# Mixing the keys of two batches by 64x64 blocks in four tiles of the array

## The chip, the cores and the metric

The kernel runs on one core of one Trainium2 chip. The metric is device time in microseconds (us) of one execution; lower is better. The kernel before takes 149.82 us, the median of three runs between 149.54 and 149.90. Engines are named as in the profile: PE is TensorE (matmuls), PEld its weight loads, DVE VectorE, ACT ScalarE, POOL GpSimd, SP SyncE, which here only issues DMAs.

## What is computed

A block-mixed attention with a gated MLP behind it, for 4 batches, 8 heads, 768 tokens and 64 channels a head. `P` is an 8x8 mixing matrix for each batch and head, made by five rounds of softmax and column normalisation:

```python
k_sorted = np.einsum('bhij,bhjcd->bhicd', P, k_b)   # 8 blocks of 96 tokens, mixed
v_sorted = np.einsum('bhij,bhjcd->bhicd', P, v_b)
scores = scale * np.matmul(q_b, k_sb.transpose(0, 1, 2, 4, 3))   # block by block
attn = softmax(scores)                               # by rows, in fp32
x = np.matmul(attn, v_sb)                            # then heads side by side: [4, 768, 512]
h = np.maximum(x @ w_in, 0.0)                        # [.., 1024], halves u and v
v_n = layernorm(v)
v_s = np.einsum('ts,bsd->btd', w_spatial, v_n) + b_spatial
out = (u * v_s) @ w_out
```

Inputs and output are fp32; the matmuls work on bf16.

## The kernel before, in words

The program is a list of small units, written out by hand or by a planner in `ORDER` and run in that order: each unit emits its instructions to the engines, and every engine works through its own queue in that order, with semaphores between them. So the order of the list is the order of each queue. A unit's name is followed by its arguments: a number of a PSUM tile (0 to 3 are pairs of banks, 10 to 17 single banks), the engine that empties it (A is ACT, D is DVE, P is POOL), the batch, and then the head pair or the piece.

The units that matter here:

- `L` (line 171) loads q, k or v of a batch with a cast to bf16, issued on POOL. A partition holds 6 tokens of each head, so a piece of the load is 6 x 64 numbers.
- `PD` (290) builds, on POOL, the mixing matrix of each head as a 128x128 block matrix: each entry of `P` times a 16x16 identity. Because a partition holds 6 tokens, a block of 96 tokens is 16 partitions.
- `KT` (402, through `mixed`, 391) mixes the keys of one head pair and turns them: 12 matmuls (line 395) with 128 rows, 64 weight columns and 128 moving columns, where the two heads of the pair use the two column halves of the array. ACT or DVE then copies the result to `kT`.
- `VM` (418, matmul 422) mixes the values, and `VC` (432) moves them to blocks of 96 tokens by DMAs on SP.
- `QT` turns q on PE (first two batches). In the third and fourth, `QP` (369) packs a head pair by a copy, and `QX` (380) turns all pairs of the batch by one transposing DMA on SP.
- `SC` (446, matmul 454, exponential 459) makes the scores of four blocks of a head pair: 64 rows, so the two heads use the two row halves of the array.
- `AT` (491, matmul 500) multiplies with the mixed values; DVE divides by the sums (507, 508). `XT` or `XD` (514) turn the result into the MLP's layout.
- `VP` and `VH` (559, 578, matmul 567) make the v half of the MLP's hidden layer, in four matmuls of 512 columns or eight of 256; `ST`, `LN`, `LA` normalise it on DVE and ACT. `UP` (605, matmul 613) makes the u half.
- `SP` (620, matmul 625) mixes over tokens, with the sum `z` on DVE (631), and `GT` (637) multiplies with u. In the last batch `SH` (676, matmul 681) and `GH` (689) do this in parts, of 512 tokens (last argument 0) and 256 (last argument 1).
- `OP`, `OE`, `OS` (645 to 669) and, for the last batch, `OH`, `OI`, `OJ` (696 to 719, matmul 701) make the output, empty it and store it. `OS` and `OJ` are DMAs on SP or ACT.
- `CK` (730), `CF` (745) and `LF` (751) are a guard. The softmax leaves out its maximum; `CK` collects on DVE whether some sum went out of range, `CF` adds this up by one matmul (747) and turns it into an integer flag on DVE (748, 749), and `LF` loads the flag into a register of every engine. At `IF` in the list every engine branches on it (815): to the rest of the list (the output of the last batch), or to a safe general path that computes all anew. With these inputs it is always the former.

```python
with tc.If(st["beyond"] < 1, preferred_fallthrough_block=False, label="usual") as usual:
    run(tail)
```

Of the kernel before, what the change touches and what calls it, by code (L numbers as in the profile page):

```python
# [34 lines left out]
UP:2:A:1:0:0 ST:1:5 AT:0:2:3:0 ST:1:4 ST:1:2 UP:1:A:1:0:1 LN:1:0:6 OP:3:0:2:2 LA:1:5 LA:1:1 SC:2:2:3:1 L:v:3:0:8
SC:0:2:2:1 PD:3:4:8 LA:1:0 OP:1:0:4:2 PD:3:0:4 LA:1:3 LA:1:2 OE:A:0:2 LA:1:4 L:k:3:0:8 QP:D:3:0 VC:2:4:8:0:4 OE:A:0:4
AT:2:2:3:1 SP:0:1:3 QP:A:3:3 AT:3:2:1:0 AT:1:2:2:1 QP:A:3:1 SP:2:1:1 AT:0:2:1:1 QP:A:3:2 VM:3:A:3:1 OP:1:0:0:2
OE:D:0:0 OS:0:0:0:1:A OS:0:0:1:2:A VM:2:A:3:3 AT:3:2:0:1 SP:0:1:2 VM:1:A:3:0 GT:P:1:1 XD:2:0 VM:3:D:3:2 SP:2:1:0
VH:16:D:2:2 QX:3:0:4 KT:0:A:3:0 KT:1:D:3:2 KT:2:D:3:3 KT:3:A:3:1 XD:2:1 VH:10:D:2:0 SC:1:3:0:1 ST:2:2 SC:3:3:0:0
SC:2:3:3:1 VC:3:4:8:0:4 OS:0:4:0:1 OS:0:4:1:2 VH:11:D:2:4 VH:10:A:2:5 AT:1:3:0:1 GT:P:1:3 VH:16:D:2:3 ST:2:3 ST:2:5  # L40
GT:P:1:2 SC:2:3:1:1 SC:0:3:2:1 SC:1:3:1:0 VH:17:A:2:1 GT:D:1:0 UP:2:A:2:1:0 AT:0:3:2:1 UP:1:A:2:1:1 ST:2:1 AT:3:3:1:1
ST:2:4 AT:2:3:3:1 UP:0:A:2:0:1 ST:2:0 UP:1:A:2:0:0 VC:3:0:4:0:4 AT:3:3:0:0 LN:2:0:6 LA:2:2 OP:0:1:0:2 OE:A:1:0 LA:2:4
AT:2:3:1:0 OP:1:1:4:2 LA:2:5 SC:3:3:2:0 LA:2:0 LA:2:3 LA:2:1 SC:0:3:3:0 OP:2:1:2:2 AT:3:3:3:0 SP:0:2:1 GT:D:2:1
OE:A:1:4 XD:3:1 AT:1:3:2:0 SP:3:2:0 SP:0:2:2 CK XD:3:0 GT:P:2:0 OE:A:1:2 SP:2:2:3 VH:1:D:3:5:3 GT:D:2:3 VH:10:D:3:4
UP:3:A:3:1:1 CF:11 VH:12:A:3:2 VH:13:A:3:1 OS:1:2:0:1 OS:1:2:1:2 LF VH:16:A:3:0 GT:D:2:2 OS:1:0:0:1:A OS:1:0:1:2:A
UP:2:A:3:1:0 ST:3:1 ST:3:3 UP:0:A:3:0:0 ST:3:4 ST:3:5 OP:1:2:0:2 ST:3:2 ST:3:0 OP:3:2:4:2 LN:3:0:6 LA:3:3 OE:D:2:0
LA:3:4 OP:2:2:2:2 LA:3:0 LA:3:1 OE:A:2:2 LA:3:5 UP:0:A:3:0:1 OE:A:2:4 LA:3:2 OS:0:2:0:1 OS:0:2:1:2 SH:12:3:2:0
SH:13:3:3:0 GH:P:3:3:0 SH:16:3:0:0 GH:D:3:2:0 SH:17:3:1:0 GH:P:3:0:0 SH:16:3:1:1 SH:12:3:2:1 OS:2:4 GH:P:3:1:0
SH:13:3:3:1 OS:2:0 GH:D:3:1:1 SH:17:3:0:1 OS:1:4 GH:D:3:3:1 OS:2:2 GH:P:3:0:1 GH:P:3:2:1 IF OH:16:3:2:0:512:0:4
OI:A:3:2:0:512 OH:12:3:3:0:512:0:4 OH:13:3:0:0:512:0:4 OI:D:3:0:0:512 OI:A:3:3:0:512 OH:17:3:1:0:512:0:4  # L50
OJ:3:2:0:512:S OJ:3:3:0:512:A OI:A:3:1:0:512 OJ:3:0:0:512:S OH:16:3:4:256:512:0:4 OI:D:3:4:256:512 OH:12:3:5:0:256:0:4
OI:D:3:5:0:256 OJ:3:1:0:512:S OJ:3:4:256:512:A OH:13:3:5:256:512:0:4 OJ:3:5:0:256:S OI:D:3:5:256:512
OH:17:3:4:0:128:0:4 OH:10:3:4:128:256:0:4 OI:B:3:4:0:256 OJ:3:5:256:512:A OJ:3:4:0:256:S
# [15 lines left out]
def kernel(  # L69
# [18 lines left out]
    TB = 128 // NB  # L88
    BH = B * H
# [670 lines left out]
    def general_path():  # L760
# [88 lines left out]
```

## Time and profile before

| | |
|---|---|
| median of three runs | 149.82 us (149.54 to 149.90) |
| span of the profiled execution | 147.7 us; its own time is not listed apart from it |
| instructions | 4114 |
| granted clock of TensorE | 1.000 |
| POOL: L293 (`PD`) | 6 of 1105 ns |
| ACT: L122, keys to `kT` | 9 of 805 ns |
| DVE: L124, keys to `kT` | 7 of 947 ns |
| loads of k, 768 KB each | 14.9 us from issue to landing (median) |

The span runs from the first to the last instruction. A row of a group gives its busy time, then the mean duration of one; the chain of waits lists, in order of time, the start, the length and the work that ended last; a row of the timeline gives start, duration, engine, line, operation and names, with the idle time before it in brackets. A matmul's duration holds the way through the array, so the distances between starts, and the lengths in the chain, tell its cost in a stream. Matmuls that use different parts of the array can run side by side; "128\*64" in a row means 128 rows by 64 columns of it.

### The profile page before, as it was taken

The page shows a single profiled execution, that of the slowest core. Times are in us where ns is not written, and L with a number is a line of the kernel's source. Part 1 is how long each engine was busy: PE and PEld are TensorE (multiplying, and loading weights), DVE is VectorE, ACT ScalarE, POOL GpSimd, SP SyncE. Part 2 cuts the span into 40 slices and gives each one's busy share as a digit, 9 for nine tenths or more (in the row PEclk, how much of TensorE's full clock was granted, in tenths as well). Part 3 has the DMA queues.
Part 4 walks back from the last instruction along what each step waited for, and adds up shares of the span by engine and source line. Part 5 has one row for each costly group of instructions (what it writes and reads, how often), then busy time and mean ns, then how long its engine had stood idle before and what let it go on. Part 6 is the DMA issues. An engine that isn't in the chain of part 4 may idle for free.

```text
span 147.7 us, 4114 instructions
## 1 busy us (share of the span) xinstructions
PE 141.4 (96%) x1691; PEld 101.0 (68%) x1691; DVE 115.1 (78%) x263; ACT 85.2 (58%) x125; POOL 39.1 (26%) x44
## 2 busy tenths in 40 slices
PE   6997999999999999999999999999999999999991
PEld 2466777857776667776877678768866876854760
DVE  3878899979987978867869879899558989846741
ACT  5357998988789447658793328756640046160040
POOL 6701994410000006991002640000002100004630
PEclk9999999999999999999999999999999999999999
DMA  2999999999999999899999999503602507007856
GB/s 60 278 204 205 204 207 201 208 225 243 227 233 231 204 200 269 131 177 211 206 202 175 213 239 278 132 0 83 28 0 60 190 2 284 0 2 266 307 210 228
DMA packets 37013, 25.93 MB, mean 176 GB/s; under 512 B 16704, under 2 KB 34112, under 8 KB 36992
## 3 DMA queue, kind: packets, MB, share of 16 engines
q0 software_dynamic: 14432, 12.19, 51.9%
q1 hardware_dynamic: 21552, 11.88, 33.8%
q10 hardware_dynamic: 1008, 1.57, 2.8%
q8 instruction: 14, 0.23, 0.6%
q14 instruction: 7, 0.06, 0.1%
HBM read 24.78 MB, written 6.29 MB: 210 GB/s over the span
## 4 chain that ended last, share of the span: by engine, by line
PE 82%; DMA 8%; DVE 5%; POOL 2%; issue 1%; ACT 1%; POOLq 0%; DVEq 0%
PE ps L625 16%; PE ps L567 15%; PE ps L613 14%; PE ps L651 11%; DMA k_in<-in_k_dram 8%; PE ps L681 5%; PE ps L500 4%; PE ps L395 4%; PE ps L701 4%; PE ps L454 4%; PE ps L422 3%; DVE x_sb L508 2%; PE ps L326 1%; PE ps L536 1%; PE ps L530 1%; DVE vb L124 1%
## 5 line engine op out<-in xcount | busy, mean ns | idle before, releaser
L642 POOL TENSOR_TENSOR gt<-z,u_sb 128x768 bf16<-128x768 f32 x7 | 11.4, 1642 | 68.0 <-DVE z L631 54.7
L459 ACT ACTIVATE ex_all<-ps 96x768 bf16<-96x768 f32 x32 | 23.7, 805 | 5.0 <-PE ps L454 4.1
L625 PE MATMUL ps<-wspT,v_sb 128*128 128x384 bf16 x144 | 25.0, 326 | 0.0
L567 PE MATMUL ps<-w_in_sb,xT 128*128 128x256 bf16 (+1 forms) x176 | 23.8, 283 | 0.0
L613 PE MATMUL ps<-xT,w_in_sb 128*128 128x384 bf16 x128 | 23.0, 326 | 0.0
L128 ACT ACTIVATE u_sb<-ps 128x768 bf16<-128x768 f32 x16 | 13.0, 811 | 17.3 <-PE ps L613 17.2
L508 DVE TENSOR_TENSOR x_sb<-ps,rec_all 96x512 bf16<-96x512 f32 x32 | 22.0, 687 | 1.1
L625 PEld LDWEIGHTS <-v_sb 128*128 128x128 bf16 x144 | 13.5, 98 | 8.4
L567 PEld LDWEIGHTS <-xT 128*128 128x128 bf16 x176 | 16.2, 98 | 4.0
L651 PE MATMUL ps<-w_out_sb,gt 128*128 128x256 bf16 x144 | 16.9, 273 | 0.0
L613 PEld LDWEIGHTS <-w_in_sb 128*128 128x128 bf16 x128 | 12.0, 98 | 7.0
L587 DVE BATCH_NORM_STATS2 stats<-v_sb 128x6 f32<-128x512 bf16 x24 | 16.2, 675 | 0.6 <-ACT v_sb L128 0.5
L122 ACT COPY o_sb<-ps 128x1024 f32<-128x1024 f32 (+2 forms) x11 | 8.9, 830 | 12.6 <-PE ps L701 9.3
L631 DVE TENSOR_TENSOR z<-ps,b_bc 128x768 f32<-128x768 f32 x12 | 11.5, 954 | 5.9 <-PE ps L625 5.1
L651 PEld LDWEIGHTS <-gt 128*128 128x128 bf16 x144 | 13.8, 98 | 2.0
L500 PEld LDWEIGHTS <-ex_all 96*128 96x128 bf16 x256 | 11.1, 97 | 2.6
L500 PE MATMUL ps<-vb,ex_all 96*128 96x65 bf16 x256 | 12.4, 193 | 0.1
L122 ACT CAST vm<-ps 128x768 bf16<-128x768 f32 x9 | 6.8, 807 | 9.7 <-PE ps L422 6.6
L694 POOL TENSOR_TENSOR gt<-z,u_sb 128x512 bf16<-128x512 f32 (+1 forms) x5 | 5.2, 1046 | 21.5 <-DVE z L687 21.5
L507 DVE RECIPROCAL rec_all<-ps 96x8 f32<-96x8 f32 x32 | 6.3, 196 | 5.5 <-PE ps L500 5.3
L130 DVE TENSOR_SCALAR v_sb<-ps 128x512 bf16<-128x512 f32 (+1 forms) x12 | 8.7, 727 | 1.7 <-PE ps L567 1.5
L236 PE MATMUL ps<-warm 128*128 128x512 bf16 (+3 forms) x38 | 8.5, 386 | 1.3 <-DVE warm L210 1.3
(100 smaller groups left out, 199.9 us busy)
## 6 DMA issues: line engine op xcount, KB each, us to landing
v_in<-in_v_dram POOLq DMA_DIRECT2D x4, 768.0 KB, 16.0
k_in<-in_k_dram POOLq DMA_DIRECT2D x4, 768.0 KB, 14.9
vb<-vm SPq DMA_DIRECT2D x24, 99.0 KB, 4.8
q_in<-in_q_dram POOLq DMA_DIRECT2D x3, 768.0 KB, 11.6
out_dram<-o_sb SPq DMA_DIRECT2D x9, 256.0 KB, 2.3
out_dram<-o_sb SPq DMA_DIRECT2D x4, 512.0 KB, 5.9
out_dram<-o_sb ACTq DMA_DIRECT2D x5, 256.0 KB, 2.3
ws_in<-in_moe_w_spatial_dram POOLq DMA_DIRECT2D x2, 576.0 KB, 18.9
```

What stands on the lines that cost most here:

```text
L122: nc.scalar.copy(out=out, in_=in_)
L128: nc.scalar.activation(out=out, in_=in_, func=AF.Relu)
L459: nc.scalar.activation(out=e_tile(b, hp, ih).rearrange("p h (x g) -> p h x g", g=G), in_=t[0:BLK, :, 0:HW].rearrange("p h (g x) -> p h x g ...
L500: nc.tensor.matmul(t[:, hh, ii * VW:ii * VW + D + 1], lhsT=e[:, c:c + 128], rhs=vb[b % 2][:, ih * NI + ii, 2 * hp + hh, 0:D + 1], start=Tr ...
L508: nc.vector.tensor_mul(out=x_sb[:, hp].rearrange("p i (h d) -> p h i d", h=2), in0=tv[:, :, :, 0:D], in1=_raw_ap(rec, 0, [rec.ap[0], [NI, ...
L567: nc.tensor.matmul(t[:, x, c:c + DH // parts], lhsT=st["xT", b][:, n // 3, kc, (n % 3) * 128:(n % 3 + 1) * 128], rhs=w_in_sb[:, kc, DH + c ...
L587: nc.vector.bn_stats(out=stats, in_=st["v_sb", b, n])
L613: nc.tensor.matmul(t[:, x, 0:HW], lhsT=w_in_sb[:, kc, mc * 128:(mc + 1) * 128], rhs=st["xT", b][:, ih, kc, :], start=(kc == 0), stop=(kc = ...
L625: nc.tensor.matmul(t[:, x, 0:HW], lhsT=st["v_sb", b, n][:, mc * 128:(mc + 1) * 128], rhs=wspT[:, 3 * x:3 * x + 3, n, :], start=(n == 0), s ...
L631: nc.vector.tensor_add(out=z.rearrange("p (x c) -> p x c", x=2), in0=t[:, :, 0:HW], in1=b_bc.rearrange("p (x c) -> p x c", x=2),)
L642: eng.tensor_mul(out=gt, in0=st["z", b, mc], in1=u)
L651: nc.tensor.matmul(t[:, x, c:c + w], lhsT=st["gt", b, mc][:, (n0 + x) * 128:(n0 + x + 1) * 128], rhs=w_out_sb[:, mc, c:c + w], start=(mc = ...
```

## The change

For the third and fourth batches k is loaded in another layout: a partition holds 12 tokens of one head, the first 64 partitions one head of a pair and the last 64 the other, so a piece is 12 x 64 numbers. A block is then 8 partitions, and the mixing matrix of a head is 64x64 (`PN` on POOL, from `prep8`, which `PS` and `PY` make on PE and DVE out of the same `P`; `M8` prepares two small constants on POOL). `KP` replaces two `KT`: 48 matmuls of 64 rows, 64 weight columns and 64 moving columns, for two head pairs, four at a time in the four 64x64 tiles of the array, each of the four into another bank. `PD` stays for the values. In the odd head pairs of these batches the two heads change places (`half`), so that all four tiles are used; q has to follow, and `QP` copies such a pair in two halves.

The order is new behind the first batch's attention; up to there `M8` is the only unit put in. The number of units of each kind stays, but for eight `KT` that become four `KP`, the new `M8`, `PS`, `PY` and two `PN`, and six `VH` that become `VP`. Many units go to another engine or place. `CF`, which stood in the fourth batch's `VH`, now stands behind the last `SH`, and `LF` behind that. `SH` gets an argument to split its matmuls, which isn't used, and the general path gets the new units.

```diff
...
-UP:3:A:3:1:1 CF:11 VH:12:A:3:2 VH:13:A:3:1 OS:1:2:0:1 OS:1:2:1:2 LF VH:16:A:3:0 GT:D:2:2 OS:1:0:0:1:A OS:1:0:1:2:A
...
-SH:13:3:3:0 GH:P:3:3:0 SH:16:3:0:0 GH:D:3:2:0 SH:17:3:1:0 GH:P:3:0:0 SH:16:3:1:1 SH:12:3:2:1 OS:2:4 GH:P:3:1:0
-SH:13:3:3:1 OS:2:0 GH:D:3:1:1 SH:17:3:0:1 OS:1:4 GH:D:3:3:1 OS:2:2 GH:P:3:0:1 GH:P:3:2:1 IF OH:16:3:2:0:512:0:4
...
+SC:0:0:0:0 L:v:1:0:8 PD:1:0:4 VB:15:D:0:3 SC:3:0:1:0 AT:1:0:2:0 SC:0:0:2:1 AT:2:0:3:0 SC:3:0:0:1 PD:1:4:8 M8
...
+ST:0:4 VP:12:A:0:1 ST:0:3 VH:10:A:0:5 L:wsb VP:13:A:0:0 PD:3:4:8 ST:0:5 WT:12:A:1 VH:16:A:0:2 ST:0:1 ST:0:0 WT:13:A:0
+PS:12 SC:0:1:3:0 PY:D VC:1:0:4 SC:2:1:0:0 WT:17:D:2 ST:0:2 LN:0:0:6 UP:1:A:0:0:0 BI AT:3:1:1:0 AT:0:1:0:0 UP:2:A:0:1:1
...
+AT:1:1:3:0 SP:0:0:1 AT:1:1:1:1 QP:A:2:3 VM:2:A:2:2 L:k:2:0:4 QP:A:2:0 SP:3:0:3 VM:0:D:2:3 QP:A:2:2 PN:2:0:4 QP:A:2:1
+PN:3:0:4 XD:1:0 VM:1:D:2:0 XD:1:1 GT:P:0:2 SP:2:0:0 KP:3:0:AA:2:1 UP:1:A:1:1:0 QX:2:0:4 VH:17:D:1:2 KP:2:0:AA:2:0
...
+LA:3:1 OE:A:2:2 LA:3:0 LA:3:3 LA:3:2 LA:3:5 OE:A:2:0 SH:11:3:1:0 SH:17:3:2:0 SH:12:3:0:0 GH:P:3:2:0 SH:14:3:0:1
+GH:D:3:0:0 OS:2:4 OS:0:2:1:2 GH:P:3:0:1 SH:16:3:3:0 GH:D:3:1:0 SH:10:3:2:1 GH:D:3:3:0 SH:12:3:1:1 OS:2:2 GH:P:3:2:1
+SH:17:3:3:1 CF:15 GH:D:3:1:1 GH:D:3:3:1 LF OS:1:0:1:2:A OS:2:0 OS:0:4:0:1 IF OH:16:3:2:0:512:0:4 OI:A:3:2:0:512
...
+        if what == "k" and int(a[0]) >= KB:
...
+            nc.gpsimd.dma_start(
+                out=st["k", b][:, lo:hi],
+                in_=_raw_ap(k, (b * H + 2 * lo) * S * D, [[GR * D, 128], [2 * S * D, hi - lo], [1, GR * D]]),
+            )
...
+    def u_PS(ps):
...
+        for i in range(NI):
+            for hh in range(2):
+                nc.tensor.matmul(
+                    parts[hh * 64:hh * 64 + 64, i], lhsT=spread8[:, i * NB:(i + 1) * NB].rearrange("p j t -> p (j t)"),
+                    rhs=turned_p[:, hh, :, KB * HP:], start=True, stop=True,
+                )
...
+    def u_PN(b, lo, hi):
+        b, lo, hi = int(b), int(lo), int(hi)
+        n = hi - lo
+        nc.gpsimd.tensor_mul(
+            out=pn(b)[:, lo:hi].rearrange("p h (i t) -> p h i t", t=TR),
...
+    def half(b, hp, hh):
+        lo = 64 * (hh ^ (hp & 1) if b >= KB else hh)
+        return slice(lo, lo + 64)
...
+    def u_KP(ps0, ps1, eng, b, m):
+        b, m = int(b), int(m)
+        ts = [ps_tile(ps0), ps_tile(ps1)]
+        for n in range(GR):
+            for row in range(2):
+                g = (n + G * row) % GR
+                for o in range(2):
+                    rows = slice(64 * row, 64 * row + 64)
+                    nc.tensor.matmul(
+                        ts[o][half(b, o, row), g // G, (g % G) * 64:(g % G) * 64 + 64],
+                        lhsT=st["k", b][rows, 2 * m + o, g * D:(g + 1) * D], rhs=pn(b)[rows, 2 * m + o, :],
+                        start=True, stop=True,
+                    )
+        for o in range(2):
+            to = turned("kT", b, 2 * m + o)[:, 0:S].rearrange("p (x b g) -> p b x g", b=2, g=G)
+            copy(eng[o], to, ts[o][:, :, 0:HW].rearrange("p b (g x) -> p b x g", g=G))
```

More of the change, by code (lines that the diff above doesn't have):

```diff
@@ L374, in u_QP @@
                 "p (k g h d) -> p k g h d", k=HP, g=G, h=2)
-        copy(
-            eng, st["qp", b][:, hp].rearrange("p g h d -> p h g d"),
-            st["q", b][:, 2 * hp:2 * hp + 2].rearrange("p h (g d) -> p h g d", g=G),
-        )
+        to, of = st["qp", b][:, hp], st["q", b][:, 2 * hp:2 * hp + 2].rearrange("p h (g d) -> p h g d", g=G)
+        if half(b, hp, 0).start == 0:
+            copy(eng, to.rearrange("p g h d -> p h g d"), of)
+        else:
+            for hh in range(2):
+                copy(eng, to[:, :, 1 - hh], of[:, hh])
     def u_QX(b, lo, hi):
@@ L452, in u_SC @@
             for hh in range(2):
-                rows = slice(hh * 64, hh * 64 + 64)
+                rows = half(b, hp, hh)
                 nc.tensor.matmul(
@@ L471, in u_SM @@
             for hh in range(2):
-                rows = slice(hh * 64, hh * 64 + 64)
+                rows = half(b, hp, hh)
                 nc.tensor.matmul(
```

119 lines of the change are left out of this document (74 added, 45 removed).

## The prediction

> **What bounds the kernel now.** I read the page first, then the busy time by stretches, then the chain of waits in order of time.
>
> ```profile
> span 147.7 us, 4114 instructions
> PE 141.4 (96%) x1691; PEld 101.0 (68%) x1691; DVE 115.1 (78%) x263; ACT 85.2 (58%) x125; POOL 39.1 (26%) x44
> PE 82%; DMA 8%; DVE 5%; POOL 2%; issue 1%; ACT 1%; POOLq 0%; DVEq 0%
> ```
>
> The chain that ended last is TensorE for 82% of the span. The three timed runs have a median of 149.82 us; the profiled execution is listed with its span alone, so about 2.1 us lie around the span, and I leave them as they are. The second view gives, for each stretch, its length and then the busy time of PE, PEld, DVE, ACT and POOL.
>
> ```profile
> 24.80:56.00 31.20, 31.15 (x405) 21.73 (x405) 26.81 (x57) 23.35 (x35) 2.27 (x3) 1.00 1.25 222
> 56.00:87.00 31.00, 31.00 (x368) 22.96 (x367) 24.05 (x48) 19.73 (x28) 15.35 (x12) 1.00 1.18 204
> 87.00:115.00 28.00, 28.00 (x346) 20.82 (x344) 23.19 (x49) 15.06 (x21) 1.64 (x1) 1.00 0.48 89
> 115.00:131.40 16.40, 16.40 (x134) 12.81 (x132) 13.76 (x35) 5.74 (x9) 0.01 (x1) 1.00 0.27 99
> 131.40:139.20 7.80, 7.80 (x50) 4.69 (x48) 4.47 (x9) 1.71 (x2) 3.75 (x3) 1.00 0.69 262
> 139.20:147.70 8.50, 5.22 (x37) 3.08 (x34) 3.38 (x9) 2.02 (x4) 1.41 (x2) 1.00 0.54 199
> ```
>
> From 24.8 us until the last matmul PE has work at every moment (31.15 of 31.20, then all of it), at a granted clock of 1.00, and every other engine has room: DVE, the fullest, is busy 26.81 of the first 31.20 us. So a microsecond of matmul taken out there is a microsecond of time, unless something makes PE wait; and any wait of PE is paid in full. The part up to 24.8 us (softmax rounds, first loads) keeps its order of units in the change, so I count nothing there. The chain in order of time then prices each kind of matmul:
>
> ```profile
> 27.68 0.79 PE ps L395 x24
> 31.05 1.83 PE ps L567 x8
> 46.27 1.95 PE ps L625 x12
> 52.85 0.65 PE ps L422 x4
> 56.98 1.46 PE ps L395 x48
> 58.44 1.41 PE ps L613 x8
> 60.72 0.62 PE ps L454 x24
> 62.31 1.30 PE ps L613 x8
> 72.03 0.45 PE ps L454 x16
> 87.33 1.46 PE ps L395 x48
> 100.95 0.24 PE ps L500 x8
> 119.44 0.10 PE ps L747
> 119.54 2.73 PE ps L567 x24
> 131.41 7.80 PE ps L681 x48
> 139.21 5.22 PE ps L701 x36
> ```
>
> **Matmuls removed.** The k mixing (L395) of the third and fourth batches goes, 48 matmuls each. Between the rows of 24 and 48, 24 more take 1.46 - 0.79 = 0.67 us: 27.9 ns each, 55.8 ns for two, which lie in two column halves of the array and run together. 96 x 27.9 = 2.68 us off the path. The rest of those rows, 0.12 us, is the price of going into another tiling; the eight L613 matmuls behind it take 1.41 instead of 1.30, so going out costs 0.11. For the scores (L454, two row halves) 8 more take 0.62 - 0.45 = 0.17 us, 21.2 ns each, and 0.11 us is left over again. I take 0.105 us for a crossing.
>
> **Matmuls added.** Each KP issues 48 matmuls of 64 rows by 64 columns with 64 moving columns, in groups of four that use four different tiles and four different banks. The nearest row for such a width is L500: 65 moving columns, one at a time, 0.24/8 = 30 ns. If four tiles run together a group costs 30 ns, twelve groups 0.36 us, four KP 1.44 us. Both weights and data must keep that pace. This row (shortest, median, longest) tells of the weights:
>
> ```profile
> L395 PE MATMUL ps<-pd,k_in x192: 219/219/243, 15.4 to 88.6; 128*64 128x128 bf16 x192
> ```
>
> The first matmul of a unit takes 243 - 219 = 24 ns more, as it waits for its own 64 weight columns; all later loads are hidden. 24 ns fits under 30 ns if the tiles load side by side, with little room. The lower end is 30 ns; the upper ends are two tiles at a time (60 ns a group, 2.88 us) and one at a time (120 ns, 5.76 us). I take 30 ns, since both pairs that the trace shows (two columns, two rows) overlap fully.
>
> [...]
>
> PS adds eight matmuls of 32 rows and 16 moving columns. Four of 32 rows and 64 columns took
>
> ```profile
> L267 PE MATMUL ps<-p_t,spread 32*128 32x64 bf16 x4 | 0.3, 190 | 0.5 <-DVE mask L224 0.5
> ```
>
> with their run-out; four pairs at 30 ns are 0.12 us (0.24 if one at a time). Crossings between tilings, counted in the two orders from the first VM of the second batch: 28 before; after, 33, since the four KP and PS stand apart from each other. 5 x 0.105 = 0.53 us. All other unit kinds keep their number; VP in place of VH is the same 2048 columns in fewer instructions. So PE's own work changes by -2.68 + 1.44 + 0.12 + 0.53 = **-0.59 us**.
>
> **The flag at the end.** The new order moves CF. CF is one matmul (L747), a reduction and a cast on DVE (L748, L749); LF then has every engine load the flag, and IF branches on it. Before, CF stands at 119.44 and PE has 24 more matmuls (to 122.27) to cover the flag:
>
> ```profile
> 119.92 0.14 DVE L748 TENSOR_REDUCE ends<-ps 1x1 f32<-1x5 f32 x1
> 120.09 0.14 DVE L749 CAST flag<-ends 1x1 int32<-1x1 f32 x1
> ```
> ```profile
> L752 PEldq TENSOR_LOAD <-flag x1: 493/493/493, 120.3 to 120.3; - x1
> ```
> ```profile
> L815 PEldq COMPARE_BRANCH  x1: 481/481/481, 137.4 to 137.4; - x1
> L815 DVEq COMPARE_BRANCH  x1: 84/84/84, 139.8 to 139.8; - x1
> ```
>
> After, CF comes behind the very last SH, and then PE's queue holds LF, the branch and the output matmuls (L701): nothing to run while it waits. Behind LF wait also DVE's copies of the output, SP's last two OS and all OJ, and one OS of ACT. CF's two DVE steps stand behind all that DVE has to do for the SH units; the steps from one DVE start to the next are in
>
> ```profile
> 135.40 0.69 DVE L687 TENSOR_TENSOR z<-ps,b_bc 128x512 f32<-128x512 f32 x1 [0.67 <-PE ps L681]
> 136.01 0.68 DVE L694 TENSOR_TENSOR gt<-z,u_sb 128x512 bf16<-128x512 f32 x1
> 136.69 0.69 DVE L687 TENSOR_TENSOR z<-ps,b_bc 128x512 f32<-128x512 f32 x1
> 138.86 0.42 DVE L687 TENSOR_TENSOR z<-ps,b_bc 128x256 f32<-128x256 f32 x1 [0.36 <-POOL gt L694]
> 139.20 0.41 DVE L694 TENSOR_TENSOR gt<-z,u_sb 128x256 bf16<-128x256 f32 x1
> ```
>
> a wide z 0.61, a wide gt 0.68, a narrow z 0.34. The 48 SH matmuls take 7.80 us in all, wide units 1.30, narrow 0.65. In the new order the wide ones are first, second, third and fifth, so the last wide one ends 5.85 us after SH begins, and its z starts 0.10 later, as 135.40 does behind 131.41 + 3.90 = 135.31. On DVE: z at 5.95, gt 6.56, narrow z 7.24, wide gt 7.58, narrow z 8.26 and 8.60, CF's reduction at 8.94. From the reduction to PE's load 120.3 - 119.92 = 0.38, the load 0.49, the branch 0.48: the first output matmul at 10.29 in place of 7.80. PE stands for **2.5 us**. Lower end: DVE has no backlog but the last z (7.90, so the reduction at 8.24) and the branch costs nothing as its target is at hand (0.08 on DVE): 8.24 + 0.38 + 0.49 = 9.11, 1.3 us. Upper end 3.2 us: two waits of a z for POOL, 0.36 us each, as the row of 138.86 has one. I take the middle, as each of its steps has its row.
>
> **Other waits.** The transposed q of the third batch (QX) is now asked for later. Before, its copies and its way were
>
> ```profile
> L122 ACT COPY qp<-q_in x7: 823/833/850, 46.8 to 77.0; 128x768 bf16<-128x768 bf16 x7
> ```
> ```profile
> qT<-qp SPq DMA_TRANSPOSE x1, 6.4
> ```
> ```profile
> L382 SPq DMA_TRANSPOSE qT<-qp x2: 3856/4064/4273, 51.8 to 80.2; - x2
> ```
>
> from 51.8 with 6.4 us to landing, and the first scores at 60.72 had 2.5 us in hand. After, three of its four copies stand on ACT behind the VM copy of a unit that PE begins at about 51.7, and PE wants the result at about 61.8 (the units of the new order added up from 31.1, where the two orders part, each at its row of the chain: L567 0.87 us, L613 1.30, L625 1.95, L422 0.33, L500 0.24, L454 0.17, L395 0.34 and the transposes at its pace, KP 0.36, and the crossings). Two of the four copies are cut in halves; an instruction more costs between 0 and 0.4 us, and I take 0.2. 52.1 + 0.83 (VM's copy, of the same size) + 0.83 + 0.83 + 1.03 puts QX at 55.6 and its landing at 62.0. I add 0.1 us, with 0 to 1.0 as ends. The new loads of k are half as many pieces of twice the length; they are needed no earlier than before, so I count nothing for them. Uncovered they would cost at most the M8, PN and PD steps put ahead of loads on POOL,
>
> ```profile
> L293 POOL TENSOR_TENSOR pd<-mask,prep_sb 128x512 bf16<-128x512 bf16 x6 | 6.5, 1105 | 7.6 <-ACT prep_sb L122 7.6
> ```
>
> 1.1 us for a PD and, by its size, about half for a PN or for M8; POOL is 26% busy, which hides them. SP's two OS behind LF send 0.75 MB more into the last stretch, which moved 199 GB/s at a DMA share of 0.54: 0 to 0.7 us, and I take 0, as the last OJ is issued over 5 us later.
>
> Sum: -0.59 + 2.5 + 0.1 = +2.0, so **151.8 us**. A measurement of this kernel can tell about 0.3%, 0.45 us, from no change.
>
> **Rivals.** *The flag does not hold PE.* If LF and the branch were passed before the flag's chain matters, only PE's own work would count: 149.82 - 0.59 = 149.2, faster. For it speaks that no wait on the flag shows on PE's path before; against it, that PE's load came 0.2 us after the cast began, as soon as there was a flag to read, and no matmul is left to cover it. The point that decides is PE's idle time between L747 and L701: under 0.15 us it is faster. Chance 0.09.
> *A short flag.* DVE arrives without backlog and the branch is free (1.3 us), the rest as bounded low, or PE loses fewer crossings: 149.82 - 0.59 + 1.0 to 1.3 = 150.2 to 150.5; around this lies no change. Chance 0.10.
> *Four tiles don't run together.* Two at a time add 2.88 - 1.44 = 1.4 us, 153.2; one at a time 4.3, 156.1. For it: no four-tile row in the trace, and 24 ns of weights against 30 ns. Against: the full overlap of both kinds of pairs. [...] Chance 0.05 for two at a time and 0.02 for anything slower, as the score pairs already run closer together than that.
>
> The forecast keeps 0.74, with its own range 150.5 to 153.0. The range of 149.9 to 153.0 takes in the short flag as well. Faster 0.09, within 0.3% 0.10, slower 0.81.
>
> **What would show it.** Right: no L395 in the last two batches, KP groups of 48 at about 0.36 us plus a crossing, PE work down by about 0.6 us, and between L747 and the first L701 a hole of some 2.5 us that ends with PE's flag load, with L748 late behind z and gt of DVE. Wrong: the L701 matmuls right behind L681 (then faster), KP at 0.7 us or more (then later still), or new PE idle time around 62 us or 80 us from q, v or vb that lands late.

## The result and the profile after

The changed kernel takes 159.97 us (median of four runs, 159.27 to 160.71) against 149.77 us: a ratio of 1.067, 95% interval 1.059 to 1.074. The forecast of 151.8 us had the sign and two of the mechanisms; 8 us of the time were not in it. A median here is over all runs of a kernel; a ratio leaves out, on both sides, the executions over 1.5% longer than the fastest of the same kernel, and the kernel before has such executions too, most of them at 153 to 155 us.

From here on the lines are those of the new file: AT is L570 (it was L500), VC L505, QX L435, the mixing KP L466, SH L753, CF L819 to L821, the flag's load L824, the branch L894, the output matmuls L773. The profiled execution took 159.27 us. Four lines of its page:

```profile
span 157.5 us, 4269 instructions
PE 145.3 (92%) x1767; PEld 99.1 (63%) x1767; DVE 114.8 (73%) x265; ACT 83.8 (53%) x126; POOL 45.5 (29%) x50
PEclk9999999999999999968999999999999999999699
PE 81%; DVE 7%; DMA 4%; POOL 2%; issue 2%; ACT 1%; DVEq 0%; POOLq 0%
```

PE was 96% busy and is 92%; the granted clock, full in every slice before, drops in two places, slices 18 and 38 of 40 (from about 67 and 146 us); and the 4% of DMA in the chain are the values `vb<-vm`, which had no share in it before (the 8% there were a load of k). The stretches (length, then busy time of PE, PEld, DVE, ACT, POOL, then the granted clock, DMA share and GB/s) say where:

```profile
24.80:56.00 31.20, 31.06 (x418) 21.86 (x415) 25.89 (x56) 24.97 (x39) 6.32 (x7) 1.00 1.22 220
56.00:87.00 31.00, 28.32 (x388) 20.77 (x387) 21.59 (x45) 16.94 (x25) 10.85 (x9) 0.94 0.95 164
87.00:115.00 28.00, 28.00 (x387) 20.21 (x386) 22.66 (x45) 15.37 (x22) 3.83 (x2) 1.00 0.46 92
115.00:135.30 20.30, 20.30 (x141) 13.04 (x140) 16.27 (x41) 6.17 (x9) 6.44 (x4) 1.00 0.49 142
135.30:143.30 8.00, 8.00 (x52) 4.70 (x49) 4.61 (x9) 1.01 (x1) 2.20 (x2) 1.00 0.36 134
143.30:157.50 14.20, 7.15 (x38) 3.49 (x37) 4.60 (x13) 2.02 (x4) 1.05 (x1) 0.87 0.54 190
```

Two stretches lost, the others are as full as before. I also added up, from the starts of all matmuls from 25 us on, the distance from each to the next beyond what a stream needs at full clock: 0.8 us before, 11.1 us after. The last matmul starts 9.5 us later (153.7 against 144.2), so PE's own work became 0.8 us less; the time went into two holes.

**The first hole, 66 to 72 us.** PE's timeline in the third batch, with what it waited for in brackets:

```profile
65.78 0.20 PE L570 MATMUL ps<-vb,ex_all 96*128 96x65 bf16 x1
66.41 0.19 PE L570 MATMUL ps<-vb,ex_all 96*128 96x65 bf16 x1 [0.44 <-DMA vb<-vm]
68.09 0.19 PE L570 MATMUL ps<-vb,ex_all 96*128 96x65 bf16 x1 [1.48 <-DMA vb<-vm]
69.03 0.44 PE L570 MATMUL ps<-vb,ex_all 96*128 96x65 bf16 x5 [0.75 <-DMA vb<-vm]
69.28 1.90 PE L637 MATMUL ps<-w_in_sb,xT 128*128 128x256 bf16 x8
```

The first AT of the third batch has its scores, but the mixed values come block by block from VC's DMAs. The starts lie 3.2 us further apart than the stream needs. In the kernel before the same eight matmuls ran without a wait:

```profile
63.45 0.41 PE L500 MATMUL ps<-vb,ex_all 96*128 96x65 bf16 x8
```

After the hole the eight matmuls of L637 take 1.90 us where eight of the kind took 1.04: until about 71.7 us they start 213 ns apart instead of 109, at half clock (granted clock 0.50 from 68.5 to 71.8 us), another 1.1 us.

**The second hole, 143 to 150 us.** PE and then DVE around the flag; the flag's load and the branch on PE:

```profile
143.27 0.17 PE L819 MATMUL ps<-bad,ones 128*1 128x5 bf16 x1
146.45 3.57 PE L773 MATMUL ps<-w_out_sb,gt 128*128 128x512 bf16 x9 [3.01 <-DVE gt L766]
150.50 3.44 PE L773 MATMUL ps<-w_out_sb,gt 128*128 128x512 bf16 x27 [0.48 <-issue]
```
```profile
141.84 0.69 DVE L759 TENSOR_TENSOR z<-ps,b_bc 128x512 f32<-128x512 f32 x1 [0.56 <-POOL gt L766]
144.63 0.43 DVE L759 TENSOR_TENSOR z<-ps,b_bc 128x256 f32<-128x256 f32 x1 [0.23 <-POOL gt L766]
144.97 0.14 DVE L820 TENSOR_REDUCE ends<-ps 1x1 f32<-1x5 f32 x1
145.14 0.14 DVE L821 CAST flag<-ends 1x1 int32<-1x1 f32 x1
```
```profile
L824 PEldq TENSOR_LOAD <-flag x1: 487/487/487, 145.3 to 145.3; - x1
```
```profile
L894 PEldq COMPARE_BRANCH  x1: 395/395/395, 145.9 to 145.9; - x1
```

The bracket names DVE's gt as the releaser, but PE sat on its own flag load until 145.8 and its branch until 146.3: this is the flag's chain, 3.2 us from start to start. Behind it the first nine output matmuls take 3.57 us, six of them at half clock, 427 ns instead of 216 between starts (granted clock 0.50 from 147.0 to 150.3 us), and then there is a stop that the profile puts down to "issue", 0.7 us by the starts. A fetch of 16 KB of code ran just before it, from 147.8 to 149.1 us, but no run shows that the stop was for code. Together 5.2 us.

### The profile page after: what moved, and what is told of

Its sections match the earlier page's. It is cut to its first block, busy times and chain, and to the rows that moved or that the text cites. A ratio compares the mean times of both kernels' runs of the same rounds, so it can differ in the third digit from the quotient of the medians.

```text
span 157.5 us, 4269 instructions
## 1 busy us (share of the span) xinstructions
PE 145.3 (92%) x1767; PEld 99.1 (63%) x1767; DVE 114.8 (73%) x265; ACT 83.8 (53%) x126; POOL 45.5 (29%) x50
## 4 chain that ended last, share of the span: by engine, by line
PE 81%; DVE 7%; DMA 4%; POOL 2%; issue 2%; ACT 1%; DVEq 0%; POOLq 0%
PE ps L695 15%; PE ps L683 13%; PE ps L637 13%; PE ps L721 10%; PE ps L250 6%; PE ps L773 4%; DMA vb<-vm 4%; PE ps L570 4%; PE ps L524 3%; PE ps L492 3%; PE ps L448 2%; POOL gt L766 2%; DVE x_sb L578 2%; PE ps L377 2%; PE ps L753 2%
## 5 line engine op out<-in xcount | busy, mean ns | idle before, releaser
L712 POOL TENSOR_TENSOR gt<-z,u_sb 128x768 bf16<-128x768 f32 x11 | 18.5, 1698 | 63.3 <-DVE z L701 57.7
L637 PE MATMUL ps<-w_in_sb,xT 128*128 128x256 bf16 (+1 forms) x148 | 23.9, 312 | 0.0
L683 PE MATMUL ps<-xT,w_in_sb 128*128 128x384 bf16 x128 | 23.7, 328 | 0.0
L125 ACT COPY o_sb<-ps 128x1024 f32<-128x1024 f32 (+2 forms) x10 | 8.1, 807 | 23.1 <-PE ps L773 13.4
L131 ACT ACTIVATE v_sb<-ps 128x512 bf16<-128x512 f32 (+1 forms) x13 | 8.2, 630 | 18.9 <-PE ps L637 18.9
L637 PEld LDWEIGHTS <-xT 128*128 128x128 bf16 x148 | 14.3, 100 | 6.2
L570 PE MATMUL ps<-vb,ex_all 96*128 96x65 bf16 x256 | 13.0, 195 | 2.8 <-DMA vb<-vm 2.7
L131 ACT ACTIVATE u_sb<-ps 128x768 bf16<-128x768 f32 x15 | 12.2, 812 | 5.8 <-PE ps L683 5.4
L570 PEld LDWEIGHTS <-ex_all 96*128 96x128 bf16 x256 | 11.5, 99 | 5.7 <-issue 3.0
L133 DVE TENSOR_SCALAR v_sb<-ps 128x512 bf16<-128x512 f32 x10 | 6.9, 691 | 7.7 <-PE ps L637 6.8
L127 DVE COPY o_sb<-ps 128x1024 f32<-128x1024 f32 (+3 forms) x8 | 5.9, 740 | 6.7 <-PE ps L773 6.1
L250 PE MATMUL ps<-warm 128*128 128x512 bf16 (+3 forms) x38 | 9.6, 419 | 1.3 <-DVE warm L224 1.3
```

The lines of the kernel that those rows point to most:

```text
L131: nc.scalar.activation(out=out, in_=in_, func=AF.Relu)
L250: nc.tensor.matmul(t[:, 0, 0:int(w)], lhsT=warm[:, 0:128], rhs=warm[:, 0:int(w)], start=True, stop=True)
L570: nc.tensor.matmul(t[:, hh, ii * VW:ii * VW + D + 1], lhsT=e[:, c:c + 128], rhs=vb[b % 2][:, ih * NI + ii, 2 * hp + hh, 0:D + 1], start=Tr ...
L637: nc.tensor.matmul(t[:, x, c:c + DH // parts], lhsT=st["xT", b][:, n // 3, kc, (n % 3) * 128:(n % 3 + 1) * 128], rhs=w_in_sb[:, kc, DH + c ...
L683: nc.tensor.matmul(t[:, x, 0:HW], lhsT=w_in_sb[:, kc, mc * 128:(mc + 1) * 128], rhs=st["xT", b][:, ih, kc, :], start=(kc == 0), stop=(kc = ...
L712: eng.tensor_mul(out=gt, in0=st["z", b, mc], in1=u)
```

## The experiments

They are told as e1 to e18, in the order in which the question moved. Lost time at a place is always the sum of distances between starts, as above. Of the order list the edits show only the units that change, with some of their neighbours; the rest of each line is left out.

### The flag, and the parts by themselves: e1 to e4

e1 puts only the test back to an early place in the changed kernel:

```diff
-VP:14:A:3:1 GT:P:2:3
+VP:14:A:3:1 CF:15 GT:P:2:3
-VP:16:A:3:4 OS:1:2:0:1
+VP:16:A:3:4 LF OS:1:2:0:1
-SH:17:3:3:1 CF:15 GH:D:3:1:1 GH:D:3:3:1 LF
+SH:17:3:3:1 GH:D:3:1:1 GH:D:3:3:1
```

> The changed kernel with two units moved: CF to behind the fourth batch's VP of tile 1, LF to behind its VP of tile 4, so that matmuls cover the flag. My theory: the hole of 3.1 us between CF's matmul and the first output matmul, and the half-clock matmuls and the second stop behind it (another 2.2 us), come from the flag alone: about 154.7 us in place of 160.0, with the L773 matmuls behind L753 within 0.9 us (the last wide gt of DVE ends 0.8 us after the last L753 began to drain). Rival: it is DVE and POOL, which finish z and gt too late in the last batch, so that PE stands there anyway: at most 1 us is gained, 159 us or more.

154.76 us, ratio 1.029 (1.022 to 1.036): 5.2 us won, and the output matmuls follow SH with two stops of 0.3 and 0.1 us. The theory held: the late test is the cause of the second hole and of what follows it. The first hole stayed.

e2 leaves the order of before and changes the mixing alone (KT to KP with M8, PS, PY, PN and the new loads):

```diff
-KT:1:A:2:0 KT:2:D:2:1 KT:3:A:2:3 KT:0:D:2:2
+KP:1:2:AD:2:0 KP:0:3:DA:2:1
-KT:0:A:3:0 KT:1:D:3:2 KT:2:D:3:3 KT:3:A:3:1
+KP:0:3:AA:3:0 KP:1:2:DD:3:1
```

> The order of the kernel before, with only the blocks changed: two adjacent KP in the place of the four KT of the third and of the fourth batch, the new loads of k, M8, PS, PY and PN put where they fit, all else in its old place. My theory: the blocks themselves are a small gain and the new order is the loss. PE work: two times 1.46 us of L395 go, two times (2 x 0.40 + 0.11) come, and PS with its crossings costs 0.33: -0.8 us, so 149.0 us. Rival: the halved copies of q, the extra POOL steps or the new loads make PE wait for q, k or vb as in the changed kernel: 151 us or more.

164.76 us, ratio 1.095 (1.089 to 1.102). The theory fell, by almost 16 us. The hole at vb is larger than in the whole change (3.3 and 1.8 us, and half clock to 75 us), and PE's branch takes 5.2 us, though the flag was loaded 17 us before it.

e3 is the other half, the new order with the old KT:

```diff
-KP:3:0:AA:2:1
+KT:3:A:2:2 KT:0:A:2:3
-KP:2:0:AA:2:0
+KT:2:A:2:0 KT:0:A:2:1
-KP:1:3:DD:3:1
+KT:1:D:3:2 KT:3:D:3:3
-KP:3:0:DA:3:0
+KT:3:D:3:0 KT:0:A:3:1
```

> The new order with the old mixing: each KP is two KT again, k is loaded whole in the old layout, and M8, PS, PY and PN are gone. My theory: the late values (PE waiting for vb at the third batch's first AT) and the late flag belong to the order: both holes stay, 160 to 161 us. Rival: the blocks bring the first hole, since two of four q copies are halved and QX comes later: without them the hole of 3 us at the third batch's first AT is under 1 us, and the time 157 us or less.

156.67 us, ratio 1.048 (1.040 to 1.055). The rival's numbers came out: 0.6 us lost at vb, no half clock there; the second hole is whole, 3.2 us. It looked as if the new code, not the order alone, made vb's delay what it is; e16 below takes that back in part, as the order with KT loses 2.4 us there too.

e4 is e1 with two loads later:

```diff
-L:wo VH:16:A:1:5 L:q:3:0:8
+L:wo VH:16:A:1:5
-L:k:3:0:4 VH:13:A:1:3
+VH:13:A:1:3
-GT:P:0:1 SC:0:2:3:1
+GT:P:0:1 L:q:3:0:8 L:k:3:0:4 SC:0:2:3:1
```

> As the kernel with the early flag, and the loads of q and k of the fourth batch are issued about 4 us later, behind the last GT of the first batch, so that the values of the third batch (VC) share the DMA engines with the load of w_out alone. My theory: these loads delay VC; the hole at the third batch's first AT shrinks from 3.2 us to 1 us or less and its half-clock stretch (1.1 us) goes: about 151.5 us. Rival: VC is late because it is queued behind the transposed q (QX): the hole stays at 2.5 us or more, and the time is that of the early flag alone, about 154.7 us.

152.57 us, ratio 1.018 (1.010 to 1.025), 0.7 us lost at vb. It looked as if the theory of the loads held; e13 below takes that back.

### Addresses: e5 to e12

What do all kernels with the new code have in common that e3 lacks? Their transposing DMAs (XD, QX), which stand ahead of VC in SP's queue, are slower. Counted from the packet records: in the kernel before and in e3 the packets of 256 bytes run at up to about 1110 in a microsecond, in the others at about 830, with 13 to 17% of the packets over 22 ns instead of 1%. The new constants (`prep8`, `spread8`, `mask8`: 128, 512 and 32 bytes a partition) stand ahead of `vm`, the load tiles, `qT`, `x_sb` and `xT`, and shift them all. Before, these start at a multiple of 256 bytes; after, at 160 modulo 256 (`vb`, at 192 modulo 256 before, is shifted too).

e5 and e7, e8 first tried a grid of 64 bytes: mask8 takes 64 bytes instead of 32, in the changed kernel, in e1 and in e2. e6 goes the other way: one unused tile of 32 bytes in the kernel before.

```diff
-    mask8 = const.tile([128, TR], BF16, name="mask8")
+    mask8 = const.tile([128, 32], BF16, name="mask8")[:, 0:TR]
```
```diff
+    pad32 = const.tile([128, 16], BF16, name="pad32")
     vm = const.tile([128, G, H, VW], BF16, name="vm")
```

> The changed kernel with one number changed: the tile mask8 is declared 32 elements wide instead of 8 (the rest unused), so that it takes 64 bytes of each partition instead of 32. In the changed kernel every tile allocated behind mask8 (vm, vb, the load tiles, qp, qT) starts at an address of 32 modulo 64; in the kernel before all of them start at a multiple of 64, and here they do again. Theory (addresses off the 64-byte grid slow the transfers into those tiles, QX's transposing ones from about 1110 to about 830 packets of 256 bytes in a microsecond, so VC behind them is late): the transposing transfers run at about 1100 packets in a microsecond again, the PE time lost before the third batch's mixing falls from 3.2 us to under 1 us, without half clock behind it: 155 to 156.5 us. Rival (the new layout of k, the halved copies or the earlier q load delay VC): transfers stay at about 830, 159 to 161 us.

> The kernel before with an unused tile of 32 bytes a partition allocated ahead of vm, and nothing else: all tiles behind it start at 32 modulo 64. Theory (addresses): transposing transfers fall to about 830 packets in a microsecond, VC and vb of the third batch land 1.5 us or more later than before, and PE loses 1 to 5 us ahead of the third batch's mixing: 151 to 156 us. Rival (addresses don't matter): 149.8 us, transfers at about 1110.

> The changed kernel with the wide mask8 and with the general-path test early (CF:15 behind VP:14:A:3:1, LF behind VP:16:A:3:4, as in the run with the early test alone, 154.8 us). Theory (addresses delay VC, the late test the rest): both holes are gone, 150.0 to 151.0 us. Rival (addresses don't matter): 154 to 155.5 us.

> The order of the kernel before with the four-tile mixing of k (the run with the blocks alone, 164.8 us) and the wide mask8. Theory (addresses): the 5 us lost before the third batch's mixing and the half clock behind them go, some 8 to 11 us; what is left is the branch of 5.2 us ahead of the output matmuls if it stays: 153 to 156 us with that branch, 148.7 to 150.0 us without it. Rival (the four-tile mixing itself or k's layout delays VC): 163 to 166 us.

e5 159.52 us (ratio 1.066), e7 155.55 (1.040, interval 1.035 to 1.045), e8 164.14 (1.095): nothing won, the grid of 64 bytes fell. But e6, the kernel before with 32 unused bytes, takes 156.76 us, ratio 1.048 (1.041 to 1.055), and stops at the very place. From the list of its waits (total, times, longest):

```profile
PE ps L501 <- DMA vb<-vm: 4.0, 3, 2.5
```

So addresses do cost 7 us here, in a program that is otherwise the same; a multiple of 64 (192 modulo 256 in e5, e7 and e8) is not enough. In e6 not all of the transposing DMAs ahead of VC are slow, but the last of them alone (25% of its 1536 packets over 22 ns): VC's first packet moves from 59.15 to 60.05 us. e9, e10 and e12 give mask8 128 bytes, so that those tiles start at a multiple of 256 again ("on the grid" from here on), in the changed kernel, in e1 and in e2; e11 puts 256 unused bytes into the kernel before.

```diff
-    mask8 = const.tile([128, TR], BF16, name="mask8")
+    mask8 = const.tile([128, 64], BF16, name="mask8")[:, 0:TR]
```
```diff
+    pad256 = const.tile([128, 128], BF16, name="pad256")
     vm = const.tile([128, G, H, VW], BF16, name="vm")
```

> The changed kernel with mask8 declared 64 elements wide (128 bytes), so that the new tiles take 768 bytes and every tile behind them starts at a multiple of 256 bytes again, as in the kernel before (there 256 modulo 512, here 0). Theory (a transposing transfer is slowed when its pieces of 256 bytes lie off the 256-byte grid: in the kernel before and in the run with the order alone none of these packets takes over 22 ns, in the shifted kernels about a fifth do, 33 to 58 ns): transposing packets at about 1100 in a microsecond again, PE time lost before the third batch's mixing under 1 us: 155 to 157 us. Rival (something else of the four-tile mixing holds them up, or any shift does): about 830 packets, 159 to 161 us.

> The same with the general-path test early, as in the run with the early test alone (154.8 us). Theory (256-byte grid): both holes gone, 150.0 to 151.5 us. Rival (not the grid): 154 to 156 us.

> The kernel before with an unused tile of 256 bytes instead of 32 (which cost 7 us): the tiles behind it move and stay on the 256-byte grid. Theory (grid): 149.5 to 150.2 us, no slow transposing packets. Rival (any shift of the addresses, or a grid of 512 bytes): 153 to 157 us.

> The order of the kernel before with the four-tile mixing of k (164.8 us with the tiles off the grid), tiles on the 256-byte grid. Theory (grid): no stop of over 1 us before the third batch's mixing; 153 to 156 us if the branch ahead of the output matmuls still takes over 5 us, 148.7 to 150 us if it doesn't. Rival (the four-tile mixing or k's layout itself): 162 to 166 us.

| tiles start at, modulo 256 | kernels | packets over 22 ns, 110 to 140 us |
|---|---|---|
| 0 | before, e3, e9 to e18 | 0 to 2.4% |
| 32 | e6 | 25% |
| 160 | after, e1, e2, e4 | 26 to 29% |
| 192 | e5, e7, e8 | 26 to 28% |

e11 takes 150.15 us, ratio 1.001 (0.996 to 1.005): a shift by 256 bytes costs nothing, one by 32 bytes 7 us. No run has a start at 128 modulo 256, so a grid of 256 bytes and one of 128 are not told apart. e12 takes 155.97 us against 164.76 without the grid, e10 152.87 (ratio 1.019, 1.014 to 1.024) against 154.76, e9 159.18 (1.055, 1.048 to 1.062) against 159.97 (1.067, 1.059 to 1.074). The packets are as the theory has them in every kernel. The times of e9 and e10 are not: they were to lose under 1 us at vb and lost 2.1 and 2.6 us. In e10:

```profile
66.62 0.19 PE L570 MATMUL ps<-vb,ex_all 96*128 96x65 bf16 x1 [0.87 <-DMA vb<-vm]
68.22 0.31 PE L570 MATMUL ps<-vb,ex_all 96*128 96x65 bf16 x5 [1.40 <-DMA vb<-vm]
```

VC starts about a microsecond sooner on the grid (first packet 59.6 us against 60.7 in the changed kernel) and is late all the same. There was a second cause.

### What VC meets: e13, e16, e17, e18

e13 is e4 on the grid (its edit and that of e9 together), e16 the same with KT for KP: e3 with CF, LF and the two loads at the places of e4.

```diff
-L:wo VH:16:A:1:5 L:q:3:0:8
+L:wo VH:16:A:1:5
-L:k:3:0:8 VH:13:A:1:3
+VH:13:A:1:3
-GT:P:0:1 SC:0:2:3:1
+GT:P:0:1 L:q:3:0:8 L:k:3:0:8 SC:0:2:3:1
```

> The changed kernel with its tiles on the 256-byte grid, the general-path test early, and the loads of q and k for the fourth batch moved behind GT:P:0:1. Theory (with the grid and the test mended, what is left before the third batch's mixing is VC sharing the DMA engines with those loads): the 2.6 us lost there at 152.9 us shrink to under 1 us: 149.3 to 150.8 us. Rival (the loads don't matter, VC is late of itself): 152 to 153.5 us.

> The new order with the old mixing of k (KT), tiles where the kernel before has them, the general-path test early and the loads of q and k for the fourth batch behind GT:P:0:1: the same as e13 without the blocks. Theory (the blocks save 0.5 to 1 us of PE work when nothing covers it): 150.0 to 151.5 us, 0.5 to 1 us above e13. Rival (the blocks save nothing, or cost): the same as e13 or below.

e13 took 154.76 us (1.030, 1.023 to 1.037), e16 153.59 (1.024, 1.021 to 1.028), with 2.7 and 2.4 us lost at vb. The theory of both fell (149.3 to 150.8 and 150.0 to 151.5 us), and e13's time lies above its rival's too (152 to 153.5). The loads of q and k are not what makes VC late, and e4's gain has no explanation of mine. e16 has no blocks, no new tiles and no slow packets and still loses 2.4 us, so the new code is not needed for the hole. What the four tiles are worth, e16 could not settle: with equal losses (4.5 us each) the last matmul starts 1.3 us sooner with them (147.0 against 148.3), but the medians say the opposite.

That leaves the third load, w_out. In the kernel before, VC's first DMA is issued at 57.59 us and w_out's load at 59.79, 2.2 us behind (first row from SP's timeline, second from POOL's); after, both at the same moment:

```profile
57.59 5.70 SPq L435 DMA_DIRECT2D vb<-vm  x8
```
```profile
59.79 0.82 POOL L194 DMA_DIRECT2D w_out_sb<-in_moe_w_out_dram  x1
```
```profile
55.20 4.09 SPq L435 DMA_TRANSPOSE qT<-qp  x1
59.38 6.23 SPq L505 DMA_DIRECT2D vb<-vm  x8
```
```profile
59.36 0.81 POOL L208 DMA_DIRECT2D w_out_sb<-in_moe_w_out_dram  x1
```

In the packet records of the changed kernel VC moves 64 packets in the microsecond from 61, then 5 and 0, while w_out moves 25, 158 and 188; in the kernel before VC has moved 367 by 62 us and w_out 11. e17 moves the load back (in e10, behind POOL's `PD`, and the two others behind GT:P:0:1); e18 moves it forward in the kernel before, by one POOL operation:

```diff
-GT:P:0:0 L:wo VH:16:A:1:5 L:q:3:0:8
+GT:P:0:0 VH:16:A:1:5
-GT:P:0:3 PD:3:0:4 ST:1:5
+GT:P:0:3 PD:3:0:4 L:wo ST:1:5
```
```diff
-GT:P:0:2 SC:1:2:3:0 VH:17:D:1:3 L:wo
+L:wo GT:P:0:2 SC:1:2:3:0 VH:17:D:1:3
```

> The changed kernel on the 256-byte grid with the early test (152.9 us) and w_out's load moved behind PD:3:0:4 of POOL (about 62.6 instead of 59.1 us), q's and k's for the fourth batch behind GT:P:0:1. Theory (VC's packets share the DMA engines with w_out's, which start as VC does): vb of the third batch lands in time, PE loses under 1 us there instead of 2.6: 149.5 to 151.0 us, unless w_out then comes late for the first output matmuls at about 70 us, which would cost up to 1 us more. Rival (VC is late whatever is loaded beside it): 152.3 to 154.8 us, 2 us or more lost at the same place.

> The kernel before with w_out's load moved one POOL operation forward (ahead of GT:P:0:2: issued at about 58.2 instead of 59.8 us, 0.6 us behind VC's issue instead of 2.2), nothing else. Theory (w_out's load beside VC): PE loses 1 to 3 us ahead of the third batch's mixing, waiting for vb: 151.5 to 154 us. Rival: 149.8 us.

Against e13, e17 moves w_out's load and nothing else. e17: 151.29 us, ratio 1.011 (1.007 to 1.016), a little over the 149.5 to 151.0 expected. With the load at 61.76 the third batch's AT run without a wait:

```profile
61.76 0.81 POOL L208 DMA_DIRECT2D w_out_sb<-in_moe_w_out_dram  x1
```
```profile
65.53 0.41 PE L570 MATMUL ps<-vb,ex_all 96*128 96x65 bf16 x8
65.77 1.04 PE L637 MATMUL ps<-w_in_sb,xT 128*128 128x256 bf16 x8
66.64 0.40 PE L570 MATMUL ps<-vb,ex_all 96*128 96x65 bf16 x8
```

e18: 155.70 us, ratio 1.033 (1.027 to 1.040), more than the 151.5 to 154 expected, for one load 1.6 us sooner:

```profile
58.21 0.82 POOL L194 DMA_DIRECT2D w_out_sb<-in_moe_w_out_dram  x1
```
```profile
64.29 0.19 PE L500 MATMUL ps<-vb,ex_all 96*128 96x65 bf16 x1 [0.62 <-DMA vb<-vm]
66.46 0.22 PE L500 MATMUL ps<-vb,ex_all 96*128 96x65 bf16 x1 [1.98 <-DMA vb<-vm]
67.65 0.44 PE L500 MATMUL ps<-vb,ex_all 96*128 96x65 bf16 x5 [0.97 <-DMA vb<-vm]
```

Taken away in the one kernel and made in the other, the hole goes and comes with w_out's load. That w_out's load can make the hole, and that moving it can take it away, is shown. That it alone decides is not. In e3 the load is issued 0.9 us behind VC and in e4 beside it, and they lost only 0.6 and 0.7 us. And the execution of e11 that was profiled took 153.49 us, though the program is the kernel before with a harmless shift, has no slow transposing packets, and issues the load 1.9 us behind VC:

```profile
57.73 6.32 SPq L436 DMA_DIRECT2D vb<-vm  x8
```
```profile
59.64 0.81 POOL L195 DMA_DIRECT2D w_out_sb<-in_moe_w_out_dram  x1
```
```profile
65.85 0.31 PE L501 MATMUL ps<-vb,ex_all 96*128 96x65 bf16 x5 [2.28 <-DMA vb<-vm]
```

PE stops for vb at the same place, and half clock follows. So the order of before stands close to this edge itself, and neither the grid nor the place of the load settles a single execution.

### Clock and code: e15, e14

e15 is e9 with 12 useless matmuls for PE to run while it waits for the flag:

```diff
-SH:17:3:3:1 CF:15 GH:D:3:1:1
+SH:17:3:3:1 CF:15 DM:13:12:512 GH:D:3:1:1
```

> The changed kernel on the grid with the late test (159.2 us) and 12 useless matmuls of 512 columns behind CF's, which PE runs while it would wait for the test. Theory (PE's clock is halved behind a hole of about 3 us because PE was idle): the output matmuls behind the branch take 216 ns from the first on, 1.5 to 2.7 us are won: 156.5 to 157.8 us, and any stop for code in the middle stays. Rival (the half clock comes of something else, such as the branch): 158.7 to 160 us.

156.89 us, ratio 1.040 (1.035 to 1.044), 2.3 us under e9. PE's timeline from CF on:

```profile
142.94 2.76 PE L250 MATMUL ps<-warm 128*128 128x512 bf16 x12
146.03 5.37 PE L773 MATMUL ps<-w_out_sb,gt 128*128 128x512 bf16 x36 [0.32 <-issue]
```

The output starts no sooner (146.03, in e9 145.58), but all 36 matmuls take 5.37 us; in e9 they took 9.3, with a stop of 0.9 us among them. PE sat idle for 0.3 us ahead of its first output matmul where it sat for 3.0 in e9: at this place its idleness is what halves the clock. The stop is gone too, against what was expected, although a fetch of 16 KB of code still falls there (at 147.4 us, in e9 at 146.9); so what makes that stop is open.

e14 is e12 with 92 more PE instructions ahead of the branch and about the same start:

```diff
-DM:10:13:512
+DM:10:6:512 DM:10:53:16
```

> The order of the kernel before with the four-tile mixing, tiles on the grid (156.0 us, with a branch of 4.5 us), and 7 of the wide warm-up matmuls of the start replaced by 53 narrow ones, so that 92 more instructions of PE lie ahead of the branch and its target lies where it does in the kernel before, modulo 256 instructions. Theory (the long branch hangs on where the target's code lies): the branch takes under 0.5 us, no hole and no half clock in the tail: 150.5 to 152 us. Rival (it hangs on something else): 155 to 157 us.

158.00 us, ratio 1.052 (1.047 to 1.058): the time is that of neither the theory nor the rival. The branch did as the theory says; e12's row, then e14's:

```profile
L894 PEldq COMPARE_BRANCH  x1: 4465/4465/4465, 139.9 to 139.9; - x1
```
```profile
L894 PEldq COMPARE_BRANCH  x1: 392/392/392, 145.9 to 145.9; - x1
```

and the tail has no hole. But at vb 3.4 us were lost instead of e12's 0.8, with half clock behind them, though w_out's load keeps its 2.4 us behind VC. Why, stays open: like the execution of e11 above, it shows that where these two streams of packets meet, small shifts elsewhere change the outcome.

## Why the prediction was wrong, step by step

**Matmuls removed and added: right.** The chain has each KP and PS as

```profile
37.31 0.22 PE ps L311 x8
56.60 0.51 PE ps L466 x48
59.39 0.51 PE ps L466 x48
92.46 0.51 PE ps L466 x48
95.69 0.51 PE ps L466 x48
```

0.51 us with the crossing, against 0.36 + 0.105; PS 0.22 against 0.12 + 0.105. The four matmuls of a group start about 3 ns apart and groups 32 ns apart, where, by the 30 ns of one L500 matmul, two tiles at a time would have shown 60 and one at a time 120: four tiles do run together, and that rival is out. PE's own work fell by 0.8 us; -0.59 was said.

**QX: right.** Issued at 55.20 (55.6 was said), and the scores at 62.10 wait for nothing. (The working left 0.2 us, 62.0 against 61.8, where the sum took 0.1.) The 0.2 us taken for a copy cut in halves had no row behind it; after, a half takes 0.51 us on ACT and a whole one 0.84, so two halves cost 0.2 more.

**The flag: right in its steps, at the upper end.** From SH's begin at 135.38 the reduction comes after 9.59 us (8.94 was said) and the first output after 11.07 (10.29). The difference is the two waits of a z for POOL, 0.56 and 0.23 us in the rows above, which stood as the upper end; the load took 0.49 us as in its row, the branch 0.40 instead of 0.48. The idle time against SH's own 7.80 us is 3.3 us; the upper end was 3.2. The rivals of a flag that does not hold PE and of a short flag are out. The stores behind LF were to cost 0 to 0.7: from the first output matmul to the span's end it is 11.0 us instead of 8.5, of which half clock and the stop behind it are 2.1, so at most 0.4 is left for them.

**Failed, first: "PE stands for 2.5 us" as the whole price of the flag.** The sum took idle time as lost once. The stop also costs what follows it: half clock (1.4 us here) and a second stop (0.7 us). e1 prices the late test at 5.2 us by the medians and 5.6 by the ratios, e10 against e9 at 6.3 and 5.4, and e15 shows by filling the stop (0.3 us idle instead of 3.0) that idleness is the cause of the half clock there. The quoted rows had a granted clock of 1.00 everywhere, so no row could price it, but the first stop of 3 us in a program that had none needed a bound for it.

How long a stop must be for half clock to follow, these traces do not tell. 3.1 to 3.2 us of one stop were enough at the flag; at vb one stop of 2.5 us (e11), three of 0.6, 1.6 and 0.9 us with matmuls between them (the changed kernel), and even two of 0.4 and 1.7 us (e9) were enough, while e10's 1.0 and 1.6 us and e16's 2.1 us at the same place left the clock full. So no single length decides in these traces.

**Failed, second: "Other waits", the term of 0.1 us.** It followed QX to the scores and ended there. SP's queue goes on: VC stands behind QX, so QX moved from 51.80 to 55.20 takes VC with it (57.59 to 59.38), and on POOL w_out's load stayed where it was. The distance between the two shrank from 2.2 us to nothing, vb of the third batch came late, and PE lost 3.2 us and 1.1 more at half clock. The last part named it ("vb that lands late"), without a price. By e17 and e18 the step is the load of w_out beside VC, with the open end that e3, e4 and e11 leave.

**Failed, third: new tiles at no cost.** The sum has no term for addresses; its "I count nothing" speaks of units and loads. The 672 bytes of new constants pushed the tiles that QX and XD read and write off their multiples of 256 bytes and slowed the transposing DMAs ahead of VC by a quarter (about 830 packets in a microsecond instead of 1110). In the whole change this is worth 0.8 us by e9's median and 1.8 by the ratios, whose intervals overlap, and 1.9 us (1.5 by the ratios) with the early test (e10); in the order of before it is worth 7 us (e6) and 9 (e12). That it is more there because w_out's load is otherwise out of VC's way fits the traces, but no run shows it.

In the table above the packets over 22 ns hardly exist at 0 (up to 2.4%) and are a quarter (25 to 29%) at 32, 160 and 192, with no step among these three. Why the start of a tile has this effect was not shown.

**The sum as it came out:** -0.8 of work, 4.3 at vb, 5.2 at the flag, the rest in small stops; 10.3 us of new losses against 0.8 won. With the test early, the tiles on the grid and w_out's load out of VC's way, e17 is left at 1.1% above the kernel before: its losses are 3.7 us instead of 0.8, now in many small stops, the largest 0.5 us each, at 75.14 us for DVE and 82.33 for v's load. No version here beats the kernel before. e2 and e12 with their long branch (5.2 and 4.5 us) show one more of these costs, for which the prediction had no term either; that the changed kernel was spared it is luck.

## What to carry to other kernels

When a step moves on a queue, follow everything queued behind it to the next wait of the bound engine, and look at what other transfer it will now meet; a margin of 2 us between two transfers can be most of the design (in e18 one load 1.6 us sooner cost 5.8 us by the medians). A stop of PE is paid twice when half clock follows it: the 3.2 us at the flag came to 5.2 us here. So price such a stop above its length, or fill it with useless matmuls (12 of them won 2.3 us in e15). Count bytes as well as instructions: see that a new constant leaves the tiles that DMAs transpose at multiples of 256 bytes, where they stood, by padding it (32 bytes cost 7 us in e6, 256 nothing in e11).

## What the hardware showed that was not expected

An unused tile of 32 bytes costs 7 us in a kernel of 150 (e6), one of 256 bytes nothing (e11). A branch of PE takes 0.39 to 0.48 us, but 5.2 us in e2 and 4.5 in e12; 92 instructions more ahead of it (e14) bring it back to 0.39. That points to the place of the code; it rests on one pair of runs, in which the branch also began 6 us later. Four matmuls of 64x64 in four tiles pass in 32 ns, 8 ns each (KP of the changed kernel). Two transfers that meet, VC at 47 to 60 ns a packet of 1056 bytes and a load at 98 ns a packet of 1024, hold each other up in a way that the same program with a shift elsewhere does not repeat (e4 and e13, e12 and e14, e11 and the kernel before); this was not cleared up.
